# A block-sparse attention with a rational feed-forward layer on one core: one query scale for a whole batch in the later batches, the last two units' output products cut by operand half and row tile, and a planner of TensorE's order that counts other engines' results as late and prefers an unchanged division of the array

## The chip, the core and the metric

The kernel runs on one core of a Trainium2 chip. The metric is the device time of one execution in microseconds (us). The core has TensorE (PE, matrix products; its weight loads are shown apart as PEld), VectorE (DVE), ScalarE (ACT), GpSimd (POOL) and SyncE (SP), which issues the DMA transfers. Each engine works through its own instructions strictly in the order in which the program was built, and waits where an instruction needs a result that is not there yet.

## The reference

The program computes a masked attention for 4 batches, 8 heads, 768 positions and 64 columns a head, and puts its output through a feed-forward layer with a rational function in the middle.

```python
scores = scale * np.matmul(q, k.transpose(0, 1, 3, 2))
mask = np.abs(blk_i - blk_j) <= 1          # blocks of 32
mask = mask | (blk_i == 0) | (blk_j == 0) | (blk_i == n_blocks - 1) | (blk_j == n_blocks - 1)
# and 3 sampled blocks for each block of queries
attn = exp(where(mask, scores, -1e9) - max) / sum
x = (attn @ v), heads side by side         # 3072 x 512
h = x @ w_in                               # 512 x 2048
P = a[0] + a[1] * h + a[2] * h2 + a[3] * h3
Q = 1.0 + np.abs(b[0]) * np.abs(h) + np.abs(b[1]) * h2
out = (P / (Q + 1e-06)) @ w_out            # 2048 x 512
```

## The kernel before

**The feed-forward part.** The 3072 rows are cut into 12 chunks of 256 rows (three for each batch). A chunk passes through 8 units, each with 256 of the 2048 middle columns, so there are 96 units. In a unit, `into` makes two blocks of 12 matmuls (lines 1121 to 1123, tile `ph`), ACT and DVE work out the rational function (lines 1128 to 1166), which ends in `gh` and its remainder `gl`, and `out_of` adds two blocks of 6 matmuls to the chunk's accumulator `acc` (lines 1177 to 1179): the 256 rows are two tiles of 128, and each tile gets gh times wo_h, gh times wo_l and gl times wo_h.

**The attention part.** It is cut into 112 parts: 22 middle query blocks of each batch with one part each, and the first and last query block with three. A part is a chain: `scores` (TensorE, 16 matmuls into `sp`, line 884; 32 in most parts of the first batch), `maxima` (DVE, two operations on `sp`, line 894), `exps` (ACT, line 912), `turn` (TensorE, 4 transposes into `pt`, line 953), a copy to `pT` (ACT, line 150), `values` (TensorE, 16 matmuls into `av`, line 1010, which the trace records as 32). After each fourth query block the results are weighted, turned (`xt`, line 1056) and stored for the chunk. The matmuls of scores and values use a quarter of the array's columns at a time (the trace names them 128\*32); all others use the whole array (128\*128). Both kinds of blocks stand between those of the feed-forward part.

**The queries.** A batch has 6 tiles of 128 queries. `prep_q` loads a tile (`ldq`, line 711), lets ACT bound its largest magnitude (line 392), and finds a power of two as its scale in `scales`: TensorE spreads the bound over the partitions (line 343, `mxq`), DVE reduces it (line 348) and makes the scale in four small operations (lines 351 to 360), and three more (lines 729 to 735) make the factors `cq` for the exponent. POOL and DVE then split the scaled tile into two half-precision parts (`hlq`, lines 154 and 386), TensorE turns them (line 741), and ACT stores them. `prep` does the same for a batch's keys and values, with one scale for a whole batch.

**The order.** `issue` is a planner that runs while the program is built. It knows a price for each operation, keeps a time for each engine, and picks again and again the operation with the smallest key: the time at which it could start, and on a tie the smallest `prio`. The program then has exactly the order in which the operations were picked. The weights are brought into their formats by DVE, ACT and POOL during the first third of the run (lines 442 to 459 and 506).

## Time and profile before

| | |
|---|---|
| median of 3 runs | 891.03 us (888.12 to 893.66) |
| time of the profiled execution | 892.74 us |
| its span, first to last instruction | 890.9 us |
| TensorE busy | 833.8 us, 94% |
| DVE busy | 737.1 us, 83% |
| ACT busy | 676.7 us, 76% |
| POOL busy | 109.9 us, 12% |
| TensorE's mean granted clock | 0.973 of full speed |

TensorE's matmuls overlap, so the duration that the trace gives for one is not what it adds to the time. What one adds is seen where matmuls follow each other without a pause: it is the distance from one start to the next. In a row of a timeline the first number is the start and the second the duration; in brackets stands the engine's idle time just before, and what ended it. In a row of waits stand the sum, the number and the longest.

### The profile page before, as it was taken

To read this page: it belongs to the slowest core of one execution; us is meant where nothing else is said; L and a number is where in the kernel's file an instruction comes from. 1 tells how busy PE (TensorE), PEld (TensorE's weight loads), DVE (VectorE), ACT (ScalarE), POOL (GpSimd) and SP (SyncE) were. 2 spreads that over 40 slices of the span, in tenths; PEclk is the share of its full clock that TensorE was granted. 3 is DMA by queue.
4 is the path that set the end of the run, shared out by engine and by line. 5 is a ranking of instruction groups with operands and counts; after the bars stand their busy time and mean duration, and the time that the engine had idled before them with its cause. 6 is when DMAs were issued, how large, how long until landed. Compare 5 with 4: busy or idle time off the path is not lost.

```text
span 890.9 us, 27280 instructions
## 1 busy us (share of the span) xinstructions
PE 833.8 (94%) x10349; PEld 646.3 (73%) x10349; DVE 737.1 (83%) x1826; ACT 676.7 (76%) x1451; POOL 109.9 (12%) x114
## 2 busy tenths in 40 slices
PE   8988686897899999899999999999999999999997
PEld 4454464675678787688877787778888777788885
DVE  5657998899999888689877978779888887788885
ACT  6777897897687878598767887898768678767563
POOL 1113631616310000100000000100000000000000
PEclk9999798798999999899999999999999999999999
DMA  7798589778856965699756965698567566640000
GB/s 201 186 169 197 169 180 207 209 199 226 177 152 160 261 184 150 149 230 230 160 147 168 277 176 148 166 235 223 152 152 179 153 172 157 165 108 24 1 24 24
DMA packets 238481, 148.01 MB, mean 166 GB/s; under 512 B 16016, under 2 KB 222736, under 8 KB 238352
## 3 DMA queue, kind: packets, MB, share of 16 engines
q1 hardware_dynamic: 238352, 146.29, 65.6%
q8 instruction: 82, 1.34, 0.7%
q14 instruction: 47, 0.39, 0.2%
HBM read 128.92 MB, written 11.01 MB: 157 GB/s over the span
## 4 chain that ended last, share of the span: by engine, by line
PE 65%; DMA 9%; DVE 9%; ACT 7%; SPq 6%; issue 3%; ACTq 0%; POOL 0%; DVEq 0%; POOLq 0%
PE acc L1177 9%; PE acc L1178 8%; PE acc L1179 8%; PE ph L1121 8%; PE ph L1122 7%; PE ph L1123 7%; PE av L1010 5%; PE sp L884 4%; PE pt L953 4%; DMA vg<-in_v_dram 3%; DMA ldq<-in_q_dram 2%; ACT pr L912 1%; ACT scrap L392 1%; DMA wl<-in_moe_w_out_dram 1%; SPq L980 1%
## 5 line engine op out<-in xcount | busy, mean ns | idle before, releaser
L1121 PE MATMUL ph<-xh,wi 128*128 128x256 f16 x768 | 213.1, 278 | 0.0
L1122 PE MATMUL ph<-xl,wi 128*128 128x256 f16 x768 | 211.9, 276 | 0.0
L1123 PE MATMUL ph<-xh,wi 128*128 128x256 f16 x768 | 211.7, 276 | 0.0
L912 ACT ACTIVATE pr<-pr,st,cq 128x256 f32<-128x256 f32 x224 | 132.2, 593 | 46.4 <-DVE st L923 46.2
L1177 PE MATMUL acc<-wo_h,gh 128*128 128x512 f32 x384 | 165.4, 431 | 0.2 <-ACT ld L150 0.2
L1179 PE MATMUL acc<-wo_h,gl 128*128 128x512 f32 x384 | 154.5, 402 | 3.5 <-DVE gl L1166 3.5
L1178 PE MATMUL acc<-wo_l,gh 128*128 128x512 f32 x384 | 153.9, 401 | 0.8 <-POOL wo_l L459 0.8
L1145 DVE SCALAR_TENSOR_TENSOR ab<-sq,absb,ab 128x512 f32<-128x512 f32 x96 | 73.7, 768 | 46.4 <-ACT ab L1142 46.3
L1128 ACT ACTIVATE sq<-ph,fc 128x512 f32<-128x512 f32 x96 | 65.5, 682 | 57.3 <-PE ph L1123 56.9
L1121 PEld LDWEIGHTS <-wi 128*128 128x128 f16 x768 | 76.2, 99 | 28.7 <-issue 15.8
L894 DVE CUSTOM_DVE_ANT_1 pr<-sp,bias 128x256 f32<-128x256 f32 x224 | 84.7, 417 | 9.4 <-PE sp L884 9.3
L1179 PEld LDWEIGHTS acc<-wo_h,gl 128*128 128x128 f32 x384 | 73.5, 191 | 22.4 <-DVE gl L1166 4.8
L1177 PEld LDWEIGHTS acc<-wo_h,gh 128*128 128x128 f32 x384 | 74.0, 193 | 17.0 <-issue 2.3
L1156 DVE SCALAR_TENSOR_TENSOR gh<-tt,par,rr 128x512 fp32r<-128x512 f32 x96 | 72.7, 757 | 14.0 <-PE acc L1178 13.4
L1178 PEld LDWEIGHTS acc<-wo_l,gh 128*128 128x128 f32 x384 | 73.9, 193 | 13.5 <-POOL wo_l L459 1.7
L154 POOL TENSOR_SCALAR hlq<-ldq,scq 128x512 f16<-128x512 f32 x24 | 21.4, 892 | 504.9 <-DVE scq L360 306.6
L1123 PEld LDWEIGHTS <-wi 128*128 128x128 f16 x768 | 76.1, 99 | 9.6
L953 PE MATMUL pt<-ident,pr 128*128 128x128 f32 x448 | 76.8, 293 | 6.1 <-ACT pT L150 4.6
L1010 PE MATMUL av<-vg,pT 128*32 128x64 f32 x3584 | 74.2, 224 | 8.8 <-DMA vg<-in_v_dram 4.8
L1122 PEld LDWEIGHTS <-wi 128*128 128x128 f16 x768 | 76.2, 99 | 8.0
L953 PEld LDWEIGHTS pt<-ident,pr 128*128 128x128 f32 x448 | 68.0, 206 | 18.3 <-ACT pT L150 6.2
L1010 PEld LDWEIGHTS av<-vg,pT 128*32 128x32 f32 x3584 | 56.4, 111 | 33.9 <-issue 10.9
(144 smaller groups left out, 1651.5 us busy)
## 6 DMA issues: line engine op xcount, KB each, us to landing
vg<-in_v_dram SPq DMA_DIRECT2D x312, 64.0 KB, 3.3
vg<-in_v_dram SPq DMA_DIRECT2D x88, 192.0 KB, 3.9
vg<-in_v_dram SPq DMA_DIRECT2D x24, 512.0 KB, 5.4
kall<-ks SPq DMA_DIRECT2D x49, 192.0 KB, 3.7
kall<-ks SPq DMA_DIRECT2D x147, 64.0 KB, 2.1
ld<-in_k_dram SPq DMA_DIRECT2D x36, 256.0 KB, 5.6
wl<-in_moe_w_in_dram SPq DMA_DIRECT2D x32, 256.0 KB, 4.8
wl<-in_moe_w_out_dram SPq DMA_DIRECT2D x16, 512.0 KB, 4.6
```

The source lines that it names most:

```text
L894: nc.vector.tensor_tensor_reduce(out=prs[x][:, g].rearrange("p (s r) -> p s r", r=BLK), in0=h["sp"][:, g].rearrange("p (s r) -> p s r", r= ...
L912: nc.scalar.activation(out=prs[x][:, g], in_=prs[x][:, g], func=AF.Exp, scale=Q["c"], bias=st[:, 6 + g:7 + g], accum_out=total if n == 1 e ...
L953: nc.tensor.transpose(pp[:, jj * P:(jj + 1) * P], cols, ident)
L1010: nc.tensor.matmul(av[rows, g], pT[:, 2 * g + kt, rows] if plain else pT[:, 2 * g + kt, pa_, rows], vf[:, g * HG + h4, kt * D:(kt + 1) * D ...
L1121: nc.tensor.matmul(o, wh, xh[:, :, cc], start=(cc == 0), stop=False)
L1122: nc.tensor.matmul(o, wh, xl[:, :, cc], start=False, stop=False)
L1123: nc.tensor.matmul(o, wl, xh[:, :, cc], start=False, stop=(cc == NCC - 1))
L1145: nc.vector.scalar_tensor_tensor(out=d["ab"], in0=d["sq"], scalar=absb[:, 1:2], in1=d["ab"], op0=ALU.mult, op1=ALU.add)
L1156: nc.vector.scalar_tensor_tensor(out=d["gh"], in0=d["tt"], scalar=par[:, 0:1], in1=d["rr"], op0=ALU.add, op1=ALU.mult)
L1177: nc.tensor.matmul(acc[:, t], ghs, wo_h[:, f], start=(new and e == 0), stop=False)
L1178: nc.tensor.matmul(acc[:, t], ghs, wo_l[:, f], start=False, stop=False)
L1179: nc.tensor.matmul(acc[:, t], gls, wo_h[:, f], start=False, stop=(last and e == 1))
```

## The change

Four things are changed.

First, the batches 2 and 3 (`b >= QB`, with QB = 2) take one query scale for the whole batch. `prep` gets a third pass (`w == 2`), which loads the batch's queries in 6 pieces of 256 KB, bounds them on ACT and runs `scales` once. Their tiles no longer run a bound, a `scales` of their own or, but for the first tile, the three operations for the factors. Batches 0 and 1 keep their tiles' scales.

Second, in the last two units of the last chunk the output block is cut anew: `piece` first issues the 8 matmuls that need only `gh`, for both row tiles, and then two matmuls with `gl` for each row tile. The copy of a row tile from the accumulator waits for that tile's last piece alone, and the first tile is copied by ACT, the second by DVE; before, both waited for the last block and were copied by ACT.

Third, the planner's choice: when it compares operations for TensorE it counts a result that comes from another engine as 1000 ns later than it expects it (`sure`), and among operations that tie it prefers by 1.0 of priority those that divide the array as the operation before did (`quarters`, set for scores and values).

Fourth, its prices: 93 ns for each change of the array's division, 600 and 450 in place of 800 and 668 for scores, 470 for 435 (turn), 580 for 560 (values), 440 for 435 (xt), 1390 for 1293 (output blocks).

```diff
-                    key = (max(t - slack, now[e]) + (0 if e == o.engs[0] else other[e]), o.prio, o.n)
+                    sure, same = max(t, o.sure[e]), e != TE or o.quarters == quarters
+                    key = (max(sure - slack, now[e]) + (0 if e == o.engs[0] else other[e]) + (0 if same else 0), o.prio - (0 if e != TE or not same else 1.0), o.n)
...
+                if o.quarters != quarters:
+                    t += 93
+                    quarters = o.quarters
...
                         x.at[y] = max(x.at[y], end + lat)
+                        x.sure[y] = max(x.sure[y], end + lat + (1000 if y == TE and e != TE else 0.0))
...
-        for w in range(2):
+        for w in ([2] if b >= QB else []) + [0, 1]:
...
+            if w == 2:
+                def largest(mx=mx):
+                    nc.vector.tensor_reduce(out=mx[0][:, 6:7], in_=mx[0][:, 0:n], axis=AX.X, op=ALU.max)
+
+                o = Op(VE, 75, largest, los, when(w, 0, n - 1))
+                q_scale[b] = scales(lambda mx=mx: mx[0][:, 6:7], "scqb", [o], when(w, 0, n - 1))
+                continue
...
-        o = Op(SC, 613, most, [o_ld], prio, uses=[s_ld])
-        o, sc = scales(lambda: d["mx"][:, 0:1], "scq", [o], prio, [s_sc])
+        if own:
+            o = Op(SC, 613, most, [o_ld], prio, uses=[s_ld])
+            o, sc = scales(lambda: d["mx"][:, 0:1], "scq", [o], prio, sl_sc)
+        else:
+            o, sc = q_scale[b]
...
+        if own or t == 0:
+            d["oc"] = row(VE, [(70, factor), (69, factor2), (69, factor3)], [o, k_scale[b]], prio, takes=d["cslot"], uses=sl_sc)
+            d["first"] = d
+        else:
+            d["first"], d["oc"] = qt[b, 0], qt[b, 0]["oc"]
...
-                o = chain["sc"] = Op(TE, 800 if near else 668, scores, deps, p, behind=chain.get("sc"), takes=[s_sp, s_pr] + ([s_st] if m == 0 else []),
+                o = chain["sc"] = Op(TE, 600 if near else 450, scores, deps, p, behind=chain.get("sc"), takes=[s_sp, s_pr] + ([s_st] if m == 0 else []),
...
-                o.work = 0.4 if near else 1.0
+                o.work, o.quarters = 0.4 if near else 1.0, True
...
+        def piece(lows, tiles):
+            def run():
+                acc = accs[c]
+                for t in tiles:
+                    for e in range(2):
+                        f = 2 * u + e
+                        gs = d["gl" if lows else "gh"][:, e * CH + t * P:e * CH + (t + 1) * P]
+                        for n, w in enumerate([wo_h] if lows else [wo_h, wo_l]):
+                            nc.tensor.matmul(acc[:, t], gs, w[:, f], start=False, stop=(last and lows and e == 1))
+            return run
...
+        if c == NC - 1 and u >= NU - 2:
+            o = chain["out"] = Op(TE, 1850, piece(False, range(CH // P)), [h], pk[11], behind=chain.get("out"), uses=[s_gh, s_acc[c]])
+            for t in range(CH // P):
+                by_tile[t] = o = chain["out"] = Op(TE, 465, piece(True, [t]), [l], pk[11], behind=chain.get("out"), uses=[s_gl, s_acc[c]])
...
-                    a = Op(among("b", SC, sc=478, ve=598), 0, copy, [o], pk[12], takes=[s_ob], uses=[acc])
+                    at = {} if not by_tile else {SC: 478} if t == 0 else {VE: 598}
+                    a = Op(at or among("b", SC, sc=478, ve=598), 0, copy, [by_tile.get(t, o)], pk[12], takes=[s_ob], uses=[acc])
```

What this does to the order is seen in three places. On TensorE, around the values block of the sixty-first part (in the third batch), the program before has, one row an instruction or a group of equal ones:

```order
L1123 LDWEIGHTS wi
L1123 MATMUL ph<-xh_118,wi 128x256
L1010 MATMUL av<-vg_109,pT 32x64 x16
L1121 LDWEIGHTS wi
L1121 MATMUL ph<-xh_118,wi 128x256
```

The changed program has at this block (its line 1035 is the values line 1010 of before, 909 the scores line 884, 1203 to 1205 the output lines 1177 to 1179):

```order
L1204 MATMUL acc<-wo_l,gh 128x512
L1205 MATMUL acc<-wo_h,gl 128x512
L1035 MATMUL av<-vg_109,pT 32x64 x16
L1035 MATMUL av<-vg_110,pT 32x64 x16
L909 LDWEIGHTS qa
L909 MATMUL sp<-kall,qa 32x256
```

The values block stood alone between two blocks of the whole array; now the next part's values follow it, and two blocks of scores follow these.

On DVE, around the fourth query tile of the third batch, the program before ends that tile's scale like this (`scq` is the tile's scale, `cq` its factors, `tt` and `gl` belong to a feed-forward unit):

```order
L359 TENSOR_SCALAR scq<-scq 128x1
L360 TENSOR_SCALAR scq<-scq 128x1
L923 TENSOR_SCALAR st<-st,cq 128x2
L729 SCALAR_TENSOR_TENSOR cq<-scq,sc_6535 128x1
L1138 SCALAR_TENSOR_TENSOR tt<-ph,fc,tt 128x512
L732 TENSOR_SCALAR cq<-cq 128x1
L386 SCALAR_TENSOR_TENSOR hlq<-ldq,scq,hlq 128x8x64
L735 TENSOR_SCALAR cq<-cq 128x1
```

The changed program has there (line 392 is 386 of before, 948 is 923, 1192 is 1166, 919 is 894; `scqb` and `cqb` are the batch's):

```order
L948 TENSOR_SCALAR st<-st,cqb 128x2
L1192 TENSOR_TENSOR gl<-tt,rr 128x512
L919 ISA pr,st<-sp,bias 128x256
L919 ISA st 128x1
L919 ISA pr,st<-sp,bias 128x256
L919 ISA st 128x1
L392 SCALAR_TENSOR_TENSOR hlq<-ldq,scqb,hlq 128x8x64
```

Only the split of the tile is left of its preparation.

At the program's end TensorE has, before, the last unit's products in this manner four times over, once for each row tile of either block:

```order
L1177 MATMUL acc<-wo_h,gh 128x512
L1178 MATMUL acc<-wo_l,gh 128x512
L1179 MATMUL acc<-wo_h,gl 128x512
L1177 MATMUL acc<-wo_h,gh 128x512
L1178 MATMUL acc<-wo_l,gh 128x512
```

In the changed program the last two units end like this, where the first row is the last unit but one's:

```order
L1218 MATMUL acc<-wo_h,gl 128x512 x4
L1218 MATMUL acc<-wo_h,gh 128x512
L1218 MATMUL acc<-wo_l,gh 128x512
L1218 MATMUL acc<-wo_h,gh 128x512
L1218 MATMUL acc<-wo_l,gh 128x512
L1218 MATMUL acc<-wo_h,gh 128x512
L1218 MATMUL acc<-wo_l,gh 128x512
L1218 MATMUL acc<-wo_h,gh 128x512
L1218 MATMUL acc<-wo_l,gh 128x512
L1218 MATMUL acc<-wo_h,gl 128x512 x4
```

The products with `gl` have moved from every third place to the end of their unit. Over the whole program TensorE's order changes the array's division 388 times before and 222 times now; behind the first `into` matmul of the seventeenth unit it is 276 and 138. TensorE has 26 transposes of line 343 where it had 36, all ten fewer behind that point.

## Rows read from the trace of the kernel before

**Rows 1.** The page's head and its busy times.

```profile
span 890.9 us, 27280 instructions
PE 833.8 (94%) x10349; PEld 646.3 (73%) x10349; DVE 737.1 (83%) x1826; ACT 676.7 (76%) x1451; POOL 109.9 (12%) x114
```

**Rows 2.** Busy time by stretch: PE, PEld, DVE, ACT, POOL, granted clock, DMA share, GB/s.

```profile
90.00:270.00 180.00, 148.44 (x2034) 113.28 (x2033) 170.45 (x403) 146.87 (x329) 70.58 (x62) 0.91 0.77 189
270.00:880.00 610.00, 602.58 (x7306) 486.09 (x7303) 506.53 (x1227) 462.72 (x955) 19.58 (x22) 0.99 0.62 158
```

**Rows 3.** Waits of PE from 270 us to the end: sum, number, longest.

```profile
PE sp L343 <- ACT scrap L392: 5.6, 2, 3.4
PE av L1010 <- ACT pT L150: 1.4, 3, 0.7
```

**Rows 4.** Timeline of PE, 404 to 407 us: start, duration, line, tiles.

```profile
404.30 0.28 PE L884 MATMUL sp<-kall,qc 128*32 128x256 f16 x4
404.51 0.28 PE L1121 MATMUL ph<-xh,wi 128*128 128x256 f16 x1
404.63 0.27 PE L1122 MATMUL ph<-xl,wi 128*128 128x256 f16 x1
...
405.72 0.27 PE L1123 MATMUL ph<-xh,wi 128*128 128x256 f16 x1
405.93 0.65 PE L1010 MATMUL av<-vg,pT 128*32 128x64 f32 x32
406.51 0.32 PE L343 MATMUL sp<-ident,mxq 128*128 128x128 f32 x1
406.67 0.27 PE L1121 MATMUL ph<-xh,wi 128*128 128x256 f16 x1
```

**Rows 5.** Timeline of PE, 315 to 316 us.

```profile
315.27 0.65 PE L1010 MATMUL av<-vg,pT 128*32 128x64 f32 x32
315.74 0.29 PE L884 MATMUL sp<-kall,qa 128*32 128x256 f16 x4
```

**Rows 6.** Groups by line: busy us, mean ns, idle before and its releaser.

```profile
L343 PE MATMUL sp<-ident,mxq 128*128 128x128 f32 x24 | 7.3, 304 | 8.5 <-ACT scrap L392 8.5
L348 DVE TENSOR_REDUCE scq<-sp 128x1 f32<-128x128 f32 x24 | 6.9, 286 | 9.9 <-PE sp L343 9.7
L894 DVE CUSTOM_DVE_ANT_1 pr<-sp,bias 128x256 f32<-128x256 f32 x224 | 84.7, 417 | 9.4 <-PE sp L884 9.3
```

**Rows 7.** Timeline of all engines, 553 to 560 us.

```profile
553.30 1.36 SPq L711 DMA_DIRECT2D ldq<-in_q_dram  x2
...
558.33 0.63 ACT L392 ACTIVATE scrap<-ldq 128x512 f16<-128x512 f32 x1 [4.79 <-DMA ldq<-in_q_dram]
...
559.10 0.32 PE L343 MATMUL sp<-ident,mxq 128*128 128x128 f32 x1 [2.23 <-ACT scrap L392]
```

**Rows 8.** Busy time by stretch, behind the two longest waits.

```profile
559.10:563.00 3.90, 3.90 (x14) 3.13 (x15) 2.39 (x8) 3.56 (x9) 0.69 (x1) 0.60 0.57 165
362.70:367.50 4.80, 4.77 (x14) 3.89 (x15) 2.66 (x10) 3.79 (x9) 0.69 (x1) 0.50 0.78 166
```

**Rows 9.** Timeline of all engines, the last 11 us.

```profile
880.21 0.68 DVE L1166 TENSOR_TENSOR gl<-tt,rr 128x512 fp32r<-128x512 f32 x1
...
880.95 0.50 PE L1179 MATMUL acc<-wo_h,gl 128*128 128x512 f32 x1 [0.81 <-DVE gl L1166]
...
881.52 0.40 PE L1178 MATMUL acc<-wo_l,gh 128*128 128x512 f32 x1
...
881.75 0.40 PE L1179 MATMUL acc<-wo_h,gl 128*128 128x512 f32 x1
...
886.39 1.08 ACT L150 ACTIVATE ld<-acc 128x512 f32<-128x512 f32 x2 [8.89 <-PE acc L1179]
```

**Rows 10.** Waits of DVE, 90 to 270 us.

```profile
DVE xn L1044 <- PE av L1010: 1.8, 2, 1.6
DVE pr L894 <- PE sp L884: 0.5, 2, 0.3
```

More of the change, by code (lines that the diff above doesn't have):

```diff
@@ L726, in factor @@
         def factor():
-            d["cc"] = p4.tile([P, 2], F32, name="cq")
+            d["cc"] = p4.tile([P, 2], F32, name="cq" if own else "cqb")
             d["c"], d["cn"] = d["cc"][:, 0:1], d["cc"][:, 1:2]
@@ L1016, in two @@
                 dv = [ol]
-                o = chain["tr"] = Op(TE, 435, turn, [oexp[m]], p, behind=chain.get("tr"), takes=[s_pt], uses=[s_pr])
+                o = chain["tr"] = Op(TE, 470, turn, [oexp[m]], p, behind=chain.get("tr"), takes=[s_pt], uses=[s_pr])
                 l = Op(among("t", SC, sc=478, ve=598), 0, whole if plain else high, [o], p, takes=[s_pT], uses=[s_pt])
@@ L1020, in two @@
                     l = Op(VE, 602, low, [l], p, uses=[s_pt, s_pT])
[L1021 removed]
+                o = chain["av"] = Op(TE, 580 if plain else 470, values, [l] + dv, p + 0.1, behind=chain.get("av"), takes=[s_av] if m == 0 else [], uses=[s_pT, s_vg] + ([] if m == 0 else [s_av]))
+                o.quarters = True
                 oval.append(o)
```

43 lines of the change are left out of this document (24 added, 19 removed).

## The prediction

> **What bounds the kernel now.** I read the page's head first: TensorE is busy for 94% of the span and no other engine for more than 83% [rows 1]. A busy share over the whole span hides stages, so the next view is the windows. There are two stages. Between 90 and 270 us DVE is busy for 170.45 of 180 us and TensorE for 148.44: there DVE sets the pace, with the weights' formats, the parts and the units all on it. From 270 us on TensorE is busy for 602.58 of 610 us and DVE for 506.53 [rows 2]: there TensorE sets it. The third view is TensorE's waits in the second stage. The two largest groups come to 7.0 us, and 5.6 of these are two waits of the query scale's transpose (line 343) for ACT's bound [rows 3]. So in 620 us nearly nothing is to be won by having operands ready sooner; what counts is how long TensorE's own instructions take. That is read from a timeline, from start to start.
>
> There a matmul of `into` follows another by 0.11 to 0.12 us (404.51, 404.63). The four scores matmuls that start at 404.30 take 0.21 until the whole array's next matmul, and the last `into` matmul takes 0.21 until the values start (405.72, 405.93). So a step from a part of the array to the whole one, or back, costs about 0.10 us more than a step without a change [rows 4]. A values block of 32 takes 0.58 us until a whole-array transpose starts (405.93 to 406.51) [rows 4], and 0.47 until scores start, which divide the array in the same way (315.27 to 315.74) [rows 5]: 0.11 less. Three places, 0.09 to 0.11 each. None of it is a wait that the profile shows; it counts as busy.
>
> **The change part by part. (a) Fewer changes of the array's division.** The order of the built program has 276 such changes behind the seventeenth unit's first matmul before, which lies about where the second window of [rows 2] begins, and 138 now: 138 fewer at 0.10 us are 13.8 us, and all of it is on TensorE's path, since TensorE doesn't wait there. The bounds are 138 times 0.09 and 0.11, 12.4 and 15.2. Another 28 changes fall away ahead of that point (388 to 222 over the program), 2.8 us; I count them at nothing, because DVE's work covers them there [rows 2], and if it didn't they would be a gain.
>
> A rule bears on this. TensorEngine Tiling (Array Packing) in the Trainium skill, section Key Properties, says that a change of the tiling mode, not of the tile, drains TensorE; the rows agree as to the kind (0.47 against 0.58). Its page TensorE: Matmul & The Clock Gate, section Step-by-step: what each phase is for, puts the drain at some 128 cycles, which at 2.4 GHz is 53 ns as an estimate; by that figure 138 changes would give 7.3 us and the time would be 6.5 us longer than my forecast. The rows have 0.09 to 0.11 and decide.
>
> **(b) The later second look.** TensorE now takes a fresh result of another engine as 1 us later, so where something else is ready it goes first. Where the planner expects a result a little too early, that shortens waits such as those of values for `pT` (1.4 us in all) [rows 3]. In the order it did: adding the start-to-start steps along the order (0.11 us for a matmul of `into`, 0.47 and 0.58 for the blocks above, 0.23 for an output matmul [rows 9]), the shortest stretch of TensorE work between a turn and its values is some 1.0 us before and 2.4 now, and between scores and turn 3.8 before and 4.5 now. So grouping two parts doesn't starve the chain by itself. I count 1.0 us for these waits, between 0 and 1.4.
>
> **(c) One query scale for batches 2 and 3.** Ten `scales` fall away (12 tiles, 2 batch scales). On TensorE each is one transpose; 406.51 to 406.67 is 0.16 us [rows 4], and its neighbours' steps are 0.11, so ten are 1.1 to 1.6; I take 1.3. On DVE each saves the reduction (286 ns) [rows 6] and seven smaller operations, four for the scale and three for the factors: at most 8 times 0.286 = 2.3 us, 23 us in all. It is worth nothing by itself, because DVE is idle for 104 us of the second window [rows 2]. ACT keeps as many bounds, 6 a batch. SP and the DMA get 12 loads of 256 KB more, 3.1 MB; at the 158 GB/s of that stage [rows 2] that is 20 us of traffic in two places where keys and values of the next batch are loaded too. The share of 0.62 leaves room, and the planner has these loads many units ahead of their use; cost nothing, or, if a gather of keys or values comes late by the one wait that such a load shows (4.8 us of ACT) [rows 7], two times some 2 us on TensorE.
>
> The two long waits are where a tile's load lands late: SP issues it at 553.30, ACT gets it at 558.33 after 4.79 us of idling, and TensorE waits 2.23 us for the bound [rows 7]. Then TensorE's granted clock is 0.60 for 3.9 us, which loses 1.6 us more [rows 8]: 3.8 us in all. This tile is of batch 2, and it no longer has a bound or a scale. But its load can still be late. POOL, which waits next, has the time (19.58 of 610 us busy) [rows 2]; the tile's split on DVE and its transposes on TensorE come after that, and TensorE's second look gives them 1 us. So the gain is between 0 and 3.8; I take half, 1.9. The other wait is 3.4 us, and the clock stands at 0.50 for 4.8 us behind it, 2.4 more [rows 3, 8]; it belongs to batch 1, whose tiles keep their scales, and I leave it where it is.
>
> **(d) The end.** At 880.95 TensorE waits 0.81 us for `gl`, while products with the next unit's `gh` would be next [rows 9]. This `gl` is done at 880.89; with all eight `gh` products first, at 0.23 us each (881.52, 881.75) [rows 9], it is there in time: 0.8 us. The two copies of the last accumulator stand one after the other on ACT, 1.08 us [rows 9]; now the first starts half a microsecond ahead of the last matmul's end and the second is one DVE operation of 128x512 like that of 880.21, 0.68 us, so 0.4 us. Together 1.2, between 0.4 (if the wait only moves to the next `gl`) and 1.5.
>
> **(e) The first stage.** DVE's work up to the last weight is the same, and the order interleaves it a little differently: it decodes some weights later and finishes the first units earlier. DVE idles for 9.6 us of these 180 [rows 2], 2.3 of them for TensorE [rows 10]. I count nothing, and keep both signs for the range: down to 9.6 us won, and some 8 lost, as much again.
>
> Sum: 13.8 + 1.0 + 1.3 + 1.9 + 1.2 = 19.2 us. From the profiled execution's 892.74 that is 873.5; this execution is 1.7 us above the median of the runs, so against the median of 891.03 I forecast **871.8 us**. The ends of the terms alone give 12.4 + 0 + 1.1 + 0 + 0.4 = 13.9 and 15.2 + 1.4 + 1.6 + 3.8 + 1.5 = 23.5, so 867 to 877.
>
> **The rivals. The first stage gains too.** DVE's 9.6 idle us [rows 2] go, because first units and fresh results are better timed: 862. For it: TensorE in this stage is short of 31 of 180 us. Against it: only 2.3 us of DVE's idling are waits for TensorE [rows 10].
>
> **The doubled blocks wait for their buffers.** Behind the seventeenth unit's first matmul the order has 27 places where scores follow scores and 14 where values follow values, 41, against 6 before: 35 more. Scores have two `sp` buffers, and others use them too; a second block can start only when DVE has been through `maxima` of an earlier one. If each of the 35 waits for one operation of `maxima`, 0.417 us [rows 6], that is 14.6 us, and the time 886: the changes saved come back as waits. Against it: DVE idles a sixth of this stage [rows 2], and the planner knows the buffers. The same Trainium skill page on tiling speaks for this rival, in its section PSUM Bottleneck: the quarter matmuls are quick and the evacuation of what they made becomes the bound; no row here shows that so far.
>
> **Slower, by the second look in the first stage.** There DVE is the bound and has nothing in hand. 31 of the 112 parts stand ahead of the last weight in DVE's order, and each goes through TensorE before DVE can have it. If TensorE puts off each by the 1 us that it now counts, and DVE has to wait for it, that costs 31 us: 903. It turns into a loss from about 19 parts on, and it would show as waits of DVE for `sp` and `av` between 90 and 270 us, which are 0.5 and 1.8 us now [rows 10]. The planner only does this where another block is ready, so most parts should lose nothing.
>
> That the change doesn't do what it says is out: the term for an unchanged division is zero in the key's first number, and works only in a tie, but 222 against 388 changes stand in the order.
>
> **How the numbers follow.** The forecast 0.68, the gain in the first stage 0.14, waits for buffers 0.12, the loss in the first stage 0.06. A difference of 1% is about what a measurement of this kernel can tell from none: 882.1 and 899.9. The forecast and the first rival are faster, but for a small part of the forecast's spread from the first stage; the buffers give no difference that can be told; so 0.82, 0.13 and 0.05. The range takes in the forecast with 8 us more from the first stage on the one side, the better part of the first rival on the other: 860 to 884.
>
> **What would show it.** In the profile after: TensorE still busy for nearly all of the second stage; values and scores of 128\*32 in one run, with 0.47 us from values to scores; 26 transposes of the scale; no wait for ACT's bound in the batches 2 and 3; no wait for `gl` at the end and one copy each on ACT and DVE. It would be wrong if the waits of scores for DVE, or of values for ACT, rose above some 10 us in the second stage, if the q tiles' transposes now wait for late loads, or if DVE between 90 and 270 us idled for more than the 9.6 us.

## The result, and the profile after

The changed kernel takes **884.24 us** (median of 5 runs, 881.36 to 887.09) against 891.03 us before (5 runs, 887.82 to 893.66): a ratio of 0.9938, with a 95% interval from 0.9914 to 0.9962. The gain is 6.8 us where 19.2 were forecast. The time lies 0.2 us above the forecast's range.

The profiled execution took 884.24 us with a span of 882.5, 8.4 us less than before. The head of the page after, which answers to [rows 1]:

```profile
span 882.5 us, 27191 instructions
PE 814.4 (92%) x10339; PEld 648.8 (74%) x10339; DVE 729.4 (83%) x1749; ACT 668.8 (76%) x1445; POOL 115.5 (13%) x119
```

TensorE is busy for 19.4 us less [rows 1]. That this is as much as the forecast's sum of 19.2 is chance: the sum held some 4 us of waits, which don't count as busy. The span is shorter by 8.4 us only, so TensorE stands idle for more of it. The windows say where (they answer to [rows 2]; columns: PE, PEld, DVE, ACT, POOL, granted clock, DMA share, GB/s):

```profile
90.00:270.00 180.00, 144.41 (x2043) 114.81 (x2042) 169.87 (x406) 144.60 (x326) 72.27 (x63) 0.91 0.77 185
270.00:880.00 610.00, 590.16 (x7295) 488.93 (x7293) 500.85 (x1145) 455.42 (x948) 19.24 (x23) 0.99 0.65 164
```

In the first stage DVE is as busy as before. In the second TensorE was busy for 602.58 of 610 us and is now for 590.16, and its work now ends at 878.0, which explains 2 us of that. What ended its waits from 270 us on (sum, number, longest; the answer to [rows 3], which had 7.0 us in its two largest groups):

```profile
PE sp L684 <- ACT kt L151: 7.7, 1, 7.7
PE pt L978 <- ACT pr L937: 4.1, 1, 4.1
PE acc L1203 <- DVE ld L1263: 2.2, 1, 2.2
PE sp L909 <- ACT kt L151: 1.5, 1, 1.5
PE ph L1147 <- DVE tt L1164: 1.1, 1, 1.1
PE pt L978 <- ACT pT L151: 1.1, 2, 0.9
```

These six come to 17.7 us. Both waits for the query scale's bound are gone, which cost 9.6 us with the slow clock behind them [rows 3, 8]. The forecast had half of one of them, 1.9 us with the slow clock behind it, and left the other, in batch 1, where it was; why that one went too isn't shown. The largest wait is new. It is one wait of 7.7 us, in the preparation of the last batch's keys. Behind it the granted clock is low (the windows of the wait and of the 15 us behind it, same columns):

```profile
576.00:585.00 9.00, 1.58 (x8) 1.05 (x7) 5.98 (x12) 3.55 (x7) 0.69 (x1) 0.76 0.80 228
585.00:600.00 15.00, 14.74 (x159) 11.38 (x159) 8.18 (x18) 10.84 (x24) 0.69 (x1) 0.80 0.75 194
```

At a clock of 0.80 the second stretch loses a fifth of 15 us, 3.0 us: this one place costs 10.7 us. Its chain is in the timeline of all engines (start, duration; in brackets the idle time before and what ended it):

```profile
570.87 0.45 SPq L546 DMA_DIRECT2D ld<-in_k_dram  x1
...
574.17 0.69 POOL L155 TENSOR_SCALAR hl<-ld,sc 128x512 f16<-128x512 f32 x1 [9.02 <-DMA ld<-in_k_dram]
574.33 1.66 SPq L596 DMA_DIRECT2D ld<-in_v_dram  x1
574.90 0.75 DVE L392 SCALAR_TENSOR_TENSOR hl<-ld,sc,hl 128x512 f16<-128x512 f32 x1 [5.25 <-POOL hl L155]
...
578.53 0.63 ACT L398 ACTIVATE scrap<-ld 128x512 f16<-128x512 f32 x1 [5.44 <-DMA ld<-in_v_dram]
...
579.43 0.40 SPq L698 DMA_DIRECT2D ks<-kt  x1
...
583.32 2.47 ACT L151 ACTIVATE kt<-sp 128x512 f16<-128x512 f16 x4 [2.88 <-DMA ks<-kt]
...
585.26 1.01 PE L684 MATMUL sp<-ident,hl 128*128 128x128 f16 x8 [7.68 <-ACT kt L151]
```

Read it backwards. TensorE's key transposes wait for ACT's copy of keys, which waits for a store of the keys before them (there is one tile `kt`) that SyncE issued at 579.43, and ACT had itself stood 5.44 us for values issued at 574.33; DVE had stood 5.25 us for POOL, and POOL 9.02 for keys issued at 570.87. All three lead to SyncE. Its own queue in that stretch:

```profile
563.48 0.39 SPq L876 DMA_DIRECT2D kall<-ks  x1
564.78 1.36 SPq L881 DMA_DIRECT2D kall<-ks  x3
566.24 0.38 SPq L999 DMA_DIRECT2D vg<-in_v_dram  x1
566.82 1.36 SPq L1005 DMA_DIRECT2D vg<-in_v_dram  x3
568.27 0.66 SPq L999 DMA_DIRECT2D vg<-in_v_dram  x1
569.15 1.68 SPq L1005 DMA_DIRECT2D vg<-in_v_dram  x3
```

It issues one transfer behind the other: the largest wait for a semaphore that it has between 550 and 585 us is 0.9 us. A set of gathers of keys (one block of neighbours, three sampled blocks, and the instructions that fetch the sampled indices between them) takes 2.76 us here, from 563.48 to 566.24; the median of 41 such sets from 270 us on is 2.91. The planner's price for such a set is 2.455 us. The page gives SyncE no busy time, since issuing isn't counted.

A full queue by itself is not new. From 520 to 576 us SyncE's own records add up to 44.7 us after and to 46.2 before. What is new is where the store of keys stands in it. After the change ACT had written these keys by 568.64, and the store was issued 10.8 us later:

```profile
567.89 0.75 ACT L151 ACTIVATE kt<-sp 128x512 f16<-128x512 f16 x1
```

Before, the same store followed its keys by 1.1 us:

```profile
570.90 2.55 ACT L150 ACTIVATE kt<-sp 128x512 f16<-128x512 f16 x4
...
574.59 0.41 SPq L682 DMA_DIRECT2D ks<-kt  x1
```

The second largest wait, 4.1 us for `pr`, leads to SyncE as well:

```profile
470.61 1.35 SPq L729 DMA_DIRECT2D ldq<-in_q_dram  x2
...
472.01 2.02 SPq L596 DMA_DIRECT2D ld<-in_q_dram  x4
...
474.36 0.69 POOL L155 TENSOR_SCALAR hlq<-ldq,scqb 128x512 f16<-128x512 f32 x1 [20.36 <-DMA ldq<-in_q_dram]
...
475.92 0.63 ACT L398 ACTIVATE scrap<-ld 128x512 f16<-128x512 f32 x1 [8.44 <-DMA ld<-in_q_dram]
...
478.04 1.29 PE L978 MATMUL pt<-ident,pr 128*128 128x128 f32 x4 [4.08 <-ACT pr L937]
```

ACT stood 8.44 us, ahead of the exponentials that TensorE waited for, for a piece of the last batch's queries: one of the loads that the batch scale adds. DVE, which hands ACT the maxima for these exponentials, stood behind POOL's split of a query tile that SyncE issued at 470.61. The clock behind this wait is 0.66 for 5 us, which loses 1.7 us more:

```profile
478.00:483.00 5.00, 4.96 (x28) 3.65 (x28) 3.25 (x6) 5.00 (x13) 0.00 (x0) 0.66 1.07 169
```

TensorE's order is as forecast. Two parts' values stand together and scores follow without the whole array between them:

```profile
466.47 1.10 PE L1035 MATMUL av<-vg,pT 128*32 128x64 f32 x64
467.38 0.29 PE L909 MATMUL sp<-kall,qa 128*32 128x256 f16 x4
```

Two blocks take 0.91 us to the next start, 0.455 each, where a block that a whole-array transpose followed took 0.58 [rows 4] and one that scores followed 0.47 [rows 5].

The end of the timeline, which answers to [rows 9]: no product waits for `gl` any more, but the two copies stand one after the other as before, and the first starts when the last four matmuls end, not ahead of that.

```profile
876.68 0.40 PE L1218 MATMUL acc<-wo_l,gh 128*128 128x512 f32 x1
...
876.91 1.10 PE L1218 MATMUL acc<-wo_h,gl 128*128 128x512 f32 x4
878.05 0.60 ACT L151 ACTIVATE ld<-acc 128x512 f32<-128x512 f32 x1 [7.80 <-PE acc L1218]
...
878.67 0.69 DVE L153 COPY ld<-acc 128x512 f32<-128x512 f32 x1 [2.68 <-ACT ld L151]
```

### The profile page after: what moved, and what is told of

Its sections match the earlier page's. It is cut to its first block, busy times and chain, and to the rows that moved or that the text cites. A ratio compares the mean times of both kernels' runs of the same rounds, so it can differ in the third digit from the quotient of the medians.

```text
span 882.5 us, 27191 instructions
## 1 busy us (share of the span) xinstructions
PE 814.4 (92%) x10339; PEld 648.8 (74%) x10339; DVE 729.4 (83%) x1749; ACT 668.8 (76%) x1445; POOL 115.5 (13%) x119
## 4 chain that ended last, share of the span: by engine, by line
PE 52%; DVE 15%; ACT 13%; DMA 10%; SPq 6%; issue 4%; POOL 0%; ACTq 0%; DVEq 0%; POOLq 0%
PE acc L1203 7%; PE acc L1205 6%; PE acc L1204 6%; PE ph L1147 6%; PE ph L1149 6%; PE ph L1148 6%; PE av L1035 4%; PE pt L978 4%; PE sp L909 3%; DMA vg<-in_v_dram 3%; ACT pr L937 3%; DVE pr L919 2%; PE acc L163 2%; ACT scrap L398 2%; ACT kt L151 2%
## 5 line engine op out<-in xcount | busy, mean ns | idle before, releaser
L1203 PE MATMUL acc<-wo_h,gh 128*128 128x512 f32 x376 | 161.2, 429 | 2.2 <-DVE ld L1263 2.2
L1205 PE MATMUL acc<-wo_h,gl 128*128 128x512 f32 x376 | 150.4, 400 | 0.0
L1204 PE MATMUL acc<-wo_l,gh 128*128 128x512 f32 x376 | 150.3, 400 | 0.0
L937 ACT ACTIVATE pr<-pr,st,cqb 128x256 f32<-128x256 f32 x112 | 66.2, 595 | 41.8 <-DVE st L948 41.8
L1148 PEld LDWEIGHTS <-wi 128*128 128x128 f16 x768 | 76.3, 99 | 15.7 <-issue 6.9
L1182 DVE SCALAR_TENSOR_TENSOR gh<-tt,par,rr 128x512 fp32r<-128x512 f32 x96 | 72.5, 755 | 16.0 <-PE acc L1204 14.2
L978 PEld LDWEIGHTS pt<-ident,pr 128*128 128x128 f32 x448 | 66.0, 206 | 22.4 <-ACT pT L151 11.9
L1035 PE MATMUL av<-vg,pT 128*32 128x64 f32 x3584 | 71.4, 224 | 8.0 <-DMA vg<-in_v_dram 5.9
L1035 PEld LDWEIGHTS av<-vg,pT 128*32 128x32 f32 x3584 | 56.5, 111 | 29.7 <-issue 19.2
L1188 DVE SCALAR_TENSOR_TENSOR tt<-tt,par,ab 128x512 f32<-128x512 f32 x96 | 74.8, 779 | 0.9
```

What stands on the lines that cost most here:

```text
L937: nc.scalar.activation(out=prs[x][:, g], in_=prs[x][:, g], func=AF.Exp, scale=Q["first"]["c"], bias=st[:, 6 + g:7 + g], accum_out=total if ...
L978: nc.tensor.transpose(pp[:, jj * P:(jj + 1) * P], cols, ident)
L1035: nc.tensor.matmul(av[rows, g], pT[:, 2 * g + kt, rows] if plain else pT[:, 2 * g + kt, pa_, rows], vf[:, g * HG + h4, kt * D:(kt + 1) * D ...
L1148: nc.tensor.matmul(o, wh, xl[:, :, cc], start=False, stop=False)
L1188: nc.vector.scalar_tensor_tensor(out=d["tt"], in0=d["tt"], scalar=par[:, 0:1], in1=d["ab"], op0=ALU.add, op1=ALU.subtract)
L1203: nc.tensor.matmul(acc[:, t], ghs, wo_h[:, f], start=(new and e == 0), stop=False)
```

## The experiments

The first theory was that the planner's new prices, or the late counting, shape an order in which TensorE waits; its rival, that any saving on TensorE is waited back, because some other engine is at its limit. To compare runs I split the time from 270 us to the start of the last matmul in three. **Own work**: each TensorE instruction that starts after 270 us at the step at which its kind follows itself in these traces (0.109 us for `into`, 0.2335 for an output matmul, 0.45 for a block of scores, 0.43 for values, some 0.12 for a transpose in f32 and 0.06 for one in f16); it grows when the first stage leaves more behind. **Changes**: their number after 270 us, counted in the trace, at 0.10 us. **Rest**: what is left, which is waits, slow clock and a constant of some us. Before it is 565.3 + 27.6 + 23.0 = 615.9 us, after 563.0 + 13.4 + 31.2 = 607.6. So the changes gave 14.2 us and the own work 2.3, and 8.2 were lost in the rest, where 4.1 had been forecast as a gain: 12.3 us, nearly all of the miss. The two places above cost 16.5 us of waits and slow clock, and the two waits for bounds that are gone gave back 9.6.

| run | median us | ratio to before (95%) | own work | changes | rest |
|---|---|---|---|---|---|
| before | 891.03 | 1 | 565.3 | 276 | 23.0 |
| the change | 884.24 | 0.9938 (0.9914 to 0.9962) | 563.0 | 134 | 31.2 |
| no preference | 900.67 | 1.0139 (1.0093 to 1.0186) | 562.2 | 279 | 31.7 |
| tile scales again | 886.94 | 0.9966 (0.9935 to 0.9997) | 564.1 | 142 | 32.0 |
| no late counting | 881.42 | 0.9906 (0.9877 to 0.9935) | 561.2 | 110 | 29.6 |
| old block prices | 886.76 | 0.9981 (0.9958 to 1.0004) | 562.4 | 122 | 32.5 |
| before + batch scale | 882.39 | 0.9926 (0.9899 to 0.9954) | 560.3 | 280 | 16.9 |
| that + new block prices | 898.38 | 1.0110 (1.0091 to 1.0128) | 576.6 | 278 | 24.8 |
| that + preference instead | 882.81 | 0.9931 (0.9898 to 0.9964) | 562.9 | 120 | 29.9 |
| copies issued by ACT | 893.45 | 1.0062 (1.0039 to 1.0084) | 569.6 | 138 | 30.9 |
| copies in four issues | 893.53 | 1.0051 (1.0029 to 1.0074) | 562.2 | 130 | 37.0 |
| copies issued by POOL | 891.74 | 1.0010 (0.9979 to 1.0040) | 567.6 | 138 | 36.5 |
| loads land 2 us later in the plan | 882.55 | 0.9928 (0.9898 to 0.9957) | 562.1 | 142 | 31.7 |
| TensorE prices x0.95 | 876.49 | 0.9874 (0.9834 to 0.9914) | 568.1 | 142 | 15.7 |
| TensorE prices x1.05 | 902.92 | 1.0151 (1.0101 to 1.0200) | 565.8 | 134 | 49.9 |
| SyncE prices x1.15 | 876.26 | 0.9824 (0.9789 to 0.9860) | 568.1 | 178 | 14.6 |
| both x1.15 and x0.95 | 874.84 | 0.9808 (0.9772 to 0.9844) | 569.2 | 224 | 10.5 |
| TensorE prices x0.91 | 876.87 | 0.9835 (0.9801 to 0.9869) | 569.1 | 214 | 12.0 |
| SyncE x1.15, no late counting | 880.04 | 0.9909 (0.9877 to 0.9940) | 563.6 | 192 | 16.8 |
| SyncE x1.15, preference 3.0 | 867.92 | 0.9774 (0.9749 to 0.9799) | 562.8 | 136 | 14.6 |

Each ratio is to the kernel before on the same chip, whose median was 891.03 us for the change and between 887.97 and 889.88 for the other runs. Where medians of different runs are compared below, up to 3 us can be the chip, and the ratios decide. The three columns behind the ratio are those of the profiled execution, which lies up to 5 us from the median of its runs, 7.8 above it for "that + new block prices". The edits below are to the changed kernel unless the text says so.

### Were the changes of division worth what was forecast?

The term without its preference; the 93 ns in the plan stay.

```diff
-                    key = (max(sure - slack, now[e]) + (0 if e == o.engs[0] else other[e]) + (0 if same else 0), o.prio - (0 if e != TE or not same else 1.0), o.n)
+                    key = (max(sure - slack, now[e]) + (0 if e == o.engs[0] else other[e]) + (0 if same else 0), o.prio, o.n)
```

> The changed kernel, but without the preference for an unchanged division (the 93 ns price stays). Its order has 282 changes from the seventeenth unit on, 144 more than the changed kernel. Theory 1 and 2 (a change costs 0.10 us): TensorE's time without waits rises by 14 us, and with the same waits the time is 895 to 901 us; with waits as before the change 886 to 891. Theory 3 (it costs much less): 880 to 886 us.

It took 900.67 us, with 145 more changes, 0.8 us less own work and nearly the same rest. By spans that is 896.6 - 882.5 = 14.1 us, by medians 16.4: 0.10 to 0.11 us a change (0.12 by the ratios). So a change of division has the price that term (a) gave it. The rest is 31.7 without the preference too, so it doesn't come from the grouped blocks alone.

### What the other parts are worth

Tile scales in all batches (`QB = 2` becomes 4), and the second look without its 1000 ns:

```diff
-    QB = 2
+    QB = 4
```

> The changed kernel, but all four batches keep a query scale for each tile (no batch pass, 12 loads of 256 KB fewer, 36 scale transposes). Its order has 146 changes of the array's division from the seventeenth unit on, against 138 in the changed kernel. Theory 1, the batch pass's loads make the key and value loads of batch 3 late and so cost the 7.7 us wait of the key transposes and the slow clock behind it: those waits go, and the time falls to 872 to 878 us. Theory 2, the planner's new order makes the loads late: such waits stay in some place, 880 to 887 us. Theory 3, a change of the division costs much less than 0.10 us and nothing was won by it: 887 to 892 us.

```diff
-                        x.sure[y] = max(x.sure[y], end + lat + (1000 if y == TE and e != TE else 0.0))
+                        x.sure[y] = max(x.sure[y], end + lat + (0.0 if y == TE and e != TE else 0.0))
```

> The changed kernel, but results of other engines count at the time at which they are expected (0 in place of 1000 ns). Its order has 110 changes of the division from the seventeenth unit on. If counting results as late protects TensorE: waits of TensorE for ACT and DVE from 270 us on rise from about 17 us to over 25 us, time 885 to 895 us. If it is itself what breaks the order: waits fall to 8 to 12 us and with 28 changes fewer (2.8 us) the time is 870 to 878 us.

The batch scale is worth 2.7 us in the changed kernel, the late counting -2.8; the intervals of both overlap that of the change, so neither is clear of noise. Neither run brings the rest down. In the first the 12 additional loads of queries are gone and the rest is 32.0 all the same: TensorE then waits in other places, the longest sum being 7.1 us of transposes for copies to `pT`.

Then the prices of the blocks, put back in the changed kernel (800 and 668 for scores, 435, 560, 435 and 1293):

```diff
-                o = chain["tr"] = Op(TE, 470, turn, [oexp[m]], p, behind=chain.get("tr"), takes=[s_pt], uses=[s_pr])
+                o = chain["tr"] = Op(TE, 435, turn, [oexp[m]], p, behind=chain.get("tr"), takes=[s_pt], uses=[s_pr])
```

> The changed kernel with the TensorE prices of before (scores 800 and 668, turn 435, values 560, xt 435, output blocks 1293); preference, 93 ns, late counting, batch scale and end stay. 124 changes of the division from the seventeenth unit on. Theory P, the new prices brought the additional waits (waits and slow clock of TensorE some 25 us in the changed kernel and three variants of it, 8 to 15 us with the old prices): they fall to 8 to 15 us, time 868 to 876 us. Theory Q, SyncE's queue is issued back to back in the stretches of preparation, and a shorter TensorE is waited back there whatever the prices: waits stay at 20 to 27 us, time 879 to 887 us.

2.5 us slower, hardly more than noise, and the rest as large: the new prices aren't what ate the gain. Then the kernel before with the batch scale as its only change (old prices and old end with it):

```diff
-                    sure, same = max(t, o.sure[e]), e != TE or o.quarters == quarters
...
+                    key = (max(t - slack, now[e]) + (0 if e == o.engs[0] else other[e]), o.prio, o.n)
...
-                if o.quarters != quarters:
-                    t += 93
-                    quarters = o.quarters
...
-        if c == NC - 1 and u >= NU - 2:
+        if False:
```

> The kernel before with the batch scale of batches 2 and 3 alone (26 scale transposes, 282 changes of the division from the seventeenth unit on). Theory 1 (the batch pass's loads cost some 10 us of waits): 893 to 900 us, with a wait of several us at the preparation of batch 3. Theory 2 (they cost nothing; the wait of 2.2 us and the slow clock go, ten transposes go): 885 to 889 us.

And this once more, with the changed kernel's block prices (600 and 450 for scores, 470, 580, 440 and 1390), still without the 93 ns, the preference and the second look:

> The kernel before with the batch scale and the new prices, without preference, 93 ns, late counting and the new end. 276 changes of the division from the seventeenth unit on; the run with the old prices gave 882.4 us and 8 us of waits and slow clock. Theory P: waits rise to 18 us or more, time 890 to 900 us. Theory Q: waits stay under 13 us, since TensorE isn't shorter, time 880 to 886 us.

The batch scale alone takes 882.39 us: by itself it gains as much as the whole change. It is the term that I had put at 1.3 + 1.9 us. By the split of the profiled executions 6.1 us of its gain are in the rest and 5.0 in own work, of which the ten transposes are 1.2; the other 3.8 is work that the first stage took over in the new order. TensorE's waits in this run, the largest two:

```profile
PE sp L905 <- ACT kt L151: 2.1, 1, 2.1
PE sp L345 <- ACT scrap L394: 1.0, 1, 1.0
```

Before, the second of these groups had 5.6 us in two waits [rows 3]. The new prices on top cost 16.0 us by the medians. The profiled execution is the slowest of its five and 23.9 us longer up to the last matmul's start: 16.3 us more of own work is left at 270 us, which is a loss in the first stage, and the rest is 7.9 us larger. Why, the runs don't show.

### Is the saving waited back?

The kernel with the batch scale alone, and the preference as the only other change:

```diff
-                    key = (max(t - slack, now[e]) + (0 if e == o.engs[0] else other[e]), o.prio, o.n)
+                    same = e != TE or o.quarters == quarters
+                    key = (max(t - slack, now[e]) + (0 if e == o.engs[0] else other[e]), o.prio - (0 if e != TE or not same else 1.0), o.n)
```

> The kernel before with the batch scale and the preference for an unchanged division alone: old prices, no 93 ns, no late counting, old end. 122 changes of the division from the seventeenth unit on, against 282 in the run with the batch scale alone, which took 882.4 us. Theory S: the prices stay short, the slack stays, waits stay near the 17 us of that run, and 160 changes less give 16 us: 864 to 872 us. Theory Q: the gain is waited back, 877 to 885 us.

It has 160 changes less, 16.0 us, and a rest that is 13.0 us larger, with 2.6 us more own work left by the first stage; 882.81 against 882.39 us. Here most of the saving is waited back, without late counting, new prices or a new end. What TensorE spends on changes that its plan doesn't price covers other engines' lateness; in the run without the preference they are priced, and cover nothing. The start times that the planner in the kernel works out fit this. Before, TensorE's `into` blocks fall ever further behind them, from 33 us at 272 us of the trace to 75 at the end. After, they go from 28 to 50, and for long stretches their distance to the plan stays level (40.2 to 40.8 us from 488 to 575); most of the growth is two steps at the two waits above, 6 us around 475 and 10 around 582.

### Who is late?

Theories were that the loads land later than planned, that SyncE has too much to issue, and that the plan's times of TensorE and of the others don't fit together. First the landing, 2 us later in the plan:

```diff
-                end = dma + 900
+                end = dma + 2900
```

> The changed kernel with every DMA expected to land 2000 ns later than before. 146 changes of the division. Theory S, with late loads as what the slack hid: waits fall to some 20 us, time 868 to 877 us. Theory Q: 880 to 888 us; if buffers that are held longer bind the plan itself, over 888 us.

882.55 us, with the waits for `kt` at 7.7 us in two pieces and a rest of 31.7: a later landing in the plan doesn't help. Then SyncE's load. Each query tile has two copies of 128 KB on chip (`qa` to `qc`); they go to ACT's queue, to POOL's, or become four on SyncE:

```diff
-            nc.sync.dma_start(out=qc[D:], in_=qa[:D])
+            nc.scalar.dma_start(out=qc[D:], in_=qa[:D])
...
-        d["oq"] = Op(SY, [(650, 131072)] * 2, swap, [x], prio, uses=[d["slot"]])
+        d["oq"] = Op(SC, [(450, 131072)] * 2, swap, [x], prio, uses=[d["slot"]])
```

> The changed kernel with the two transfers that copy a query tile's halves (qa to qc, 24 tiles) issued by ACT, behind its own evacuation, in place of SyncE. SyncE has 48 issues of some 0.5 us fewer. Theory Q: waits from 270 us on fall by 5 us or more, time 872 to 879 us. Theory P: no fall beyond the scatter of a newly dealt order, 881 to 888 us.

```diff
-        d["oq"] = Op(SY, [(650, 131072)] * 2, swap, [x], prio, uses=[d["slot"]])
+        d["oq"] = Op(SY, [(650, 65536)] * 4, swap, [x], prio, uses=[d["slot"]])
```

> The changed kernel with each of these copies cut in two, so that SyncE issues four transfers a tile in place of two: 48 issues of some 0.5 us more, the same bytes. Theory Q: waits rise by 5 us or more, time 889 to 897 us. Theory P: 881 to 888 us.

```diff
-            nc.sync.dma_start(out=qc[D:], in_=qa[:D])
+            nc.gpsimd.dma_start(out=qc[D:], in_=qa[:D])
...
-        d["oq"] = Op(SY, [(650, 131072)] * 2, swap, [x], prio, uses=[d["slot"]])
+        d["oq"] = Op(PO, [(650, 131072)] * 2, swap, [x], prio, uses=[d["slot"]])
```

> The changed kernel with the two copies of a query tile's halves issued by GpSimd, which is idle from 270 us on for 590 of 610 us, in place of SyncE. 138 changes of the division. Theory S1: SyncE has 48 issues fewer and waits less for ACT; waits of TensorE fall by 5 us or more, 873 to 880 us. Theory S2, or a slow issue on GpSimd: 881 to 890 us.

Four issues cost 9.3 us by the medians and 4.6 by the spans, with a rest that is 5.8 us larger. But 48 issues less on SyncE don't help: 893.45 and 891.74 us. In both the first stage leaves some 5 to 7 us more behind; the rest stays on ACT's queue (30.9) and grows on POOL's (36.5). TensorE's waits with the copies on POOL:

```profile
PE sp L909 <- ACT kt L151: 5.7, 2, 3.8
PE pt L978 <- ACT pr L937: 4.8, 2, 2.8
PE av L1035 <- DMA vg<-in_v_dram: 4.7, 4, 2.3
```

An issue that leaves SyncE also leaves its plan, so the planner puts other loads there as tightly as before: between 520 and 576 us SyncE issues 78 and 79 transfers in these two runs and 79 in the changed kernel. So the queue is as full as it was; that this is the whole reason isn't shown.

So the fit of the plan was changed by itself, with the same instructions: TensorE's prices, where the plan has its clock at full speed.

```diff
                 if not warm:
                     price *= 2 if price > 1100 or price < 500 else 1.8
+                else:
+                    price *= 0.95
```

> The changed kernel with all of the planner's TensorE prices times 0.95 once the clock is up. 142 changes of the division from the seventeenth unit on. Theory S: the planner of before priced TensorE too short (its changes of the division cost nothing), so that TensorE came later than planned to everything and the lateness of loads and of ACT was hidden; the exact prices take that slack away. Then the waits and slow clock from 270 us on fall from 31 us by this reckoning to some 20, time 868 to 877 us. Theory Q: SyncE, DVE or ACT set the pace in the stretches of preparation whatever the plan; waits stay at 27 to 35 us, time 880 to 888 us.

The other way, `price *= 1.05`:

> The same with the TensorE prices times 1.05. 134 changes of the division. Theory S: waits rise to 38 us or more, time 889 to 898 us. Theory Q: 880 to 888 us.

The rest is 15.7, 31.2 and 49.9 us at 0.95, 1 and 1.05. The slower TensorE stands in the plan, the later the others may be there, and the more the real TensorE waits for them. At 1.05 the waits are spread over all of them:

```profile
PE pt L980 <- ACT pT L151: 8.5, 9, 2.5
PE pt L980 <- ACT pr L939: 5.2, 2, 3.1
PE sp L686 <- ACT kt L151: 4.6, 3, 1.9
PE sp L911 <- ACT qa L765: 3.8, 1, 3.8
PE sp L686 <- DVE st L921: 3.4, 2, 2.6
```

Last, SyncE's prices alone. Between 520 and 576 us of the changed kernel SyncE's issues take some 50 us in the trace, its waits left out, where the plan's own figures have 44.0, some 1.15 times as long, while TensorE keeps to its plan until the wait.

```diff
-                    t = max(t, lanes.pop(0) if e == SY else t) + ns
+                    t = max(t, lanes.pop(0) if e == SY else t) + 1.15 * ns
```

> The changed kernel with SyncE's prices for issuing transfers times 1.15 in the plan, the ratio between 520 and 576 us (50.6 us on the chip for 44.0 planned). 178 changes of the division from the seventeenth unit on. Theory S1, SyncE's queue is what comes late: waits and slow clock from 270 us on fall from 31 to some 20 us; with 4 us for 44 changes more, 874 to 880 us. Theory S2, ACT and DVE are late by themselves: waits stay at 28 to 34 us, 884 to 892 us.

876.26 us, 8.0 less than the change (10 by the ratios), with the rest at 14.6. TensorE's waits from 270 us on:

```profile
PE sp L759 <- DVE hlq L392: 1.4, 1, 1.4
PE sp L1082 <- DVE st L919: 1.3, 1, 1.3
PE sp L909 <- ACT kt L151: 0.7, 1, 0.7
```

Of the wait of 7.7 us for `kt` nothing is left (the 0.7 is scores'), and the store of keys follows them by 0.9 us again:

```profile
573.22 0.78 ACT L151 ACTIVATE kt<-sp 128x512 f16<-128x512 f16 x1
...
574.90 0.40 SPq L698 DMA_DIRECT2D ks<-kt  x1
```

SyncE's queue is no emptier (46.6 us of records from 520 to 576): the new price changed the order and the plan's times, not the load. A price that fits for one engine, off the path and never counted as busy, gives what 5% for all engines against TensorE gave. Whether a higher price for ACT or DVE would have done the same wasn't tried. Both together, and TensorE's prices at 0.91:

> SyncE's prices times 1.15 and TensorE's times 0.95. 224 changes of the division. If both make the same slack: waits near the 16 us of the run with TensorE times 0.95 and 8 us more for 82 changes, 880 to 888 us. If they add up: waits under 12 us, 872 to 879 us.

> TensorE's prices times 0.91 in place of 0.95, SyncE's as they were. 214 changes of the division, 72 more than with 0.95. Theory S1 and S2: waits fall a little further, to 10 to 15 us, and the changes cost 7 us: 877 to 885 us, no better than 0.95.

874.84 and 876.87 us: the rest falls to 10.5 and 12.0, but the changes rise to 224 and 214 and the first stage leaves 6 us more behind; nothing that is clear of noise is won over SyncE's prices alone. With SyncE's prices the late counting was taken out, and apart from that the preference raised from 1.0 to 3.0:

> SyncE's prices times 1.15, and no late counting (0 in place of 1000 ns). 192 changes of the division from the seventeenth unit on, 14 more than with late counting. If late counting is what keeps TensorE's waits down: waits over 20 us, 883 us or more. If the right SyncE prices do it alone: waits at 13 to 17 us, 876 to 880 us.

```diff
-                    key = (max(sure - slack, now[e]) + (0 if e == o.engs[0] else other[e]) + (0 if same else 0), o.prio - (0 if e != TE or not same else 1.0), o.n)
+                    key = (max(sure - slack, now[e]) + (0 if e == o.engs[0] else other[e]) + (0 if same else 0), o.prio - (0 if e != TE or not same else 3.0), o.n)
```

> SyncE's prices times 1.15, with the preference for an unchanged division at 3.0 of priority in place of 1.0. 136 changes of the division from the seventeenth unit on, 42 fewer. If the waits stay at 14 to 17 us: 4 us less, 870 to 874 us. If the gain is waited back: 875 to 880 us.

Without the late counting it is 880.04 us; with SyncE's prices right it seems to be worth some 4 us by the medians (the profiled executions' spans, 874.8 and 875.7 us, don't show it), where it cost 2.8 without. The stronger preference has 136 changes as in the changed kernel, and a rest of 14.6: **867.92 us**, the fastest of all, 20.1 us less than the kernel before on that chip and, by the ratios, some 15 less than the change. Its second stage, and its largest waits there:

```profile
270.00:850.00 580.00, 575.48 (x7302) 478.07 (x7300) 491.43 (x1129) 452.13 (x942) 20.95 (x26) 1.00 0.68 172
```

```profile
PE sp L1082 <- DVE st L919: 1.2, 1, 1.2
PE sp L759 <- DVE st L919: 1.1, 2, 0.9
```

The same savings, most of them no longer waited back. Each edit deals the whole order anew, and the own work alone varies from 560 to 577 us by that, so one run says little. But the six runs that give TensorE shorter or SyncE longer prices have a rest of 10.5 to 16.8 us, and the eleven others with the preference or with the changes priced have 29.6 to 49.9.

## Why the prediction was wrong

**What bounds the kernel, and the step that failed.** TensorE set the second stage before; that was right. But its plan had no price for the 276 changes, and this kept it behind the plan and behind the others. I read from 7 us of waits that nobody else was near the limit. They showed that the others were in time for a TensorE slowed by 28 us of changes, not for one without them. **The step that failed** is in term (a), "all of it is on TensorE's path, since TensorE doesn't wait there": the sum has no term for savings that are waited back. Where the preference is added to the batch scale alone, 13.0 of the 16.0 us that it saves come back as waits and slow clock. In the change itself 8.2 us were lost in the rest, where the sum had a gain of 4.1 (1.0 in (b), 1.9 in (c), 1.2 in (d)).

**(a) The changes of division**: right in size and place, wrong in that all of it would reach the time. 13.8 us forecast, 14.2 by the count in the trace, 14.1 to 16.4 by the run without the preference.

**(b) The later second look**: 1.0 us forecast. The waits of values for `pT` (1.4 us) are gone, but transposes now wait 1.1 us for the same copies, so nothing is left of the gain.

**(c) The batch scale**: "The share of 0.62 leaves room, and the planner has these loads many units ahead of their use; cost nothing" failed too. The DMA engines did have room over the whole stage (0.65), though none where these queries load (1.02 from 474 to 478 us). SyncE, which issues every load one by one, was full in the preparation of a batch, before as after, and the plan believed it some 13% quicker than it is. One of the additional loads held ACT up for 8.44 us and cost TensorE 5.8 us with the slow clock. The keys of the last batch cost 10.7. My upper bound, two times 2 us, was taken from the one late load that showed before. These loads aren't the whole reason, though: without them (tile scales again) the rest is as large, and with them in the order of before (batch scale alone) it is 16.9 us. What would have shown the full queue in the profile of before is a timeline of SyncE's queue alone, which I didn't ask for; it would not have shown by itself that a quicker TensorE has to wait for it. The gain of the batch scale itself I had too small: alone it is worth 6.8 us (882.39 against 889.16 for the kernel before on the same chip), against 3.2, though a part of this is the new order's and not the scale's.

**(d) The end**: the wait of 0.81 us for `gl` is gone, as forecast. The copies gave nothing: they take 1.31 us from 878.05 to 879.36, where the two on ACT took 1.08. The first was to start half a microsecond ahead of the last matmul's end and starts at that end; DVE's copy starts when ACT's is done. Why is not shown.

**(e) The first stage**: right. DVE's busy time is 169.87 against 170.45 us, and the own work left behind fell by 2.3 us, of which the ten transposes are 1.2.

**The rivals.** The time is close to that of the rival of the doubled blocks, 886 us, but not by its mechanism: no wait of scores for DVE's `st` stands among the largest after, where it had 14.6 us for them. Its outcome was right (the changes saved come back as waits), its place wrong; I gave 0.12 to it, and none to a loader that is late. That the range was missed by 0.2 us only is luck: its upper end stood for a loss in the first stage. The gain in the first stage and the loss there didn't happen. At 0.82 for faster by over 1% I was too sure of a sum in which nobody else could become late.

**What stays open.** Whether it is SyncE's price as such, or any price that leaves the others more time, that brings the rest down; why moving issues to ACT or POOL makes the kernel slower; whether the late counting gains or loses (2.8 us one way, 4 the other); and how much of the rest at 14.6 us could still go.

## What to carry to other kernels

When the engine that sets the pace gets faster, ask of each other engine how late it may be now, and count the queue that issues the DMAs among them: look at its timeline, since it has no busy share, and look at where in it the transfer stands that the bound engine needs next. In a plan that is built from prices, an operation without a price on the bound engine is slack for all others; who prices it or removes it should first make the others' prices true. Here 14 us of real savings showed as 7, and one factor on SyncE's prices, with a preference that had room to work, brought the gain to 20.

## What the hardware showed

A change of the array's division costs 0.10 to 0.11 us, measured over 145 changes, half of them each way, and counts as busy. A plain issue on SyncE takes 0.3 to 0.6 us by the medians of the kernel's lines, a set of sampled gathers of keys 2.9 (median of 41), and two 128 KB copies 0.56 + 0.52 us on POOL. Landing took 3.7 us from an issue by SyncE, 4.0 by ACT and 4.7 by POOL (medians of 48), so the other queues were no better for these copies.
